# Two sums over partitions in an attention and MLP block: block transposes in place of a strided pass through DRAM, with a new order table

## The chip, the core and the metric

One of the eight cores of a Trainium2 chip runs the whole program. It has a matrix engine (TensorE, PE in the profile; its weight loads stand apart as PEld), a vector engine (VectorE, DVE), an activation engine (ScalarE, ACT), a slower general engine (GpSimd, POOL) and a sequencer (SyncE, SP) that here issues almost all transfers. Sixteen DMA engines carry the transfers. Each engine executes its own list of instructions strictly in order and waits for the others by semaphores, so an instruction that has to wait holds everything behind it on its engine. The metric is the device time of one execution in microseconds (us), lower is better.

## What is computed

The reference is a block with 2,048 tokens of width D = 576, cut here to its lines:

```
mod = (silu(c) @ w_mod).reshape(1, 6, 1, 576)      # c: 1 x 576, w_mod: 576 x 3456
sa, ca, ga, sb, cb, gb = mod[:, 0] ... mod[:, 5]
h = layernorm(x) * (1 + ca) + sa
x = x + ga * linear_attention(h, wqkv, wo)         # 32 heads of 18, kv and z summed over all tokens
h = layernorm(x) * (1 + cb) + sb
x = x + gb * (silu(h @ w1) @ w2)                   # F = 4608
```

The six modulation vectors come from one row times a 576 x 3456 matrix. The kernel takes them in three pieces of 1,152 columns: piece 0 (sa, ca) at the very start, and the later pieces 1 (ga, sb) and 2 (cb, gb) during the attention. The change concerns pieces 1 and 2.

## The kernel before

The first half of the program, called stage A here, works through the 16 tiles of 128 tokens in four blocks of four. For each tile the PE makes the k and q projections (line 928, into the banks psK), DVE and ACT apply the feature map (lines 935 to 941 and 494), and the PE adds up kv sums (line 1053, into the banks psG, from which ACT or DVE moves them to `sum`, lines 1061 to 1065). Every next block is layer-normalised, turned by DVE block transposes (line 1020) and a pass through DRAM (lines 1026 to 1035), modulated (lines 359 and 361) and split into a high and a low part (lines 996 and 997). At the end of stage A come the kv products (line 1186), a mask (line 1193), the products with wo (line 1223) and then the attention output and the MLP.

`mod_steps` (line 1090) makes pieces 1 and 2. Five times it loads 128 rows of w_mod (line 434), ACT scales each row by its silu(c) (lines 1099 and 1101), and POOL adds the result to `tmod` (line 1103). Then `tmod` holds 128 partial rows of 1,152 numbers that still have to be summed over the partitions. Before the change that is done through DRAM: SP stores `tmod` to `parts` (line 1104), the ACT queue fetches it back so that each partition gets 9 columns of all 128 rows, in pieces of 36 bytes (line 1107), DVE sums with a strided read (line 1110), and SP stores the 1,152 sums to `vec` (line 1111). From `vec` come the columns and rows that later work reads: `col_b`, `bc_ga`, `bc_gb` (lines 754, 1117, 1119, 1122), the bounds (line 757 and `find_bounds`), and with them the scale factors of the MLP (`find_factors`, lines 731 to 744).

Where things lie: the w_mod rows are loaded in turn into four rooms, two of them the accumulator rows of tiles 4 to 7 (`acc`), which q tiles 4 to 7 need later, and two the buffers `raw2`. The fetched `parts` lie in one `raw2` buffer. The buffer `crow` holds the sums.

Two tables set orders. `STAGE_A` gives the order in which the program text of stage A is emitted; the change doesn't touch it. `ORDERS` gives for each engine the order in which its instructions run: a list of indices, where index n is the n-th instruction emitted for that engine. Before the change it covers the first 2,991 PE, 656 DVE, 489 ACT, 262 POOL and 203 SP instructions, which is the program up to about 445 us; what is not listed follows in the order of emission. An instruction's place below is its position in such a list.

Of the kernel before, what the change touches and what calls it, by code (L numbers as in the profile page):

```python
# [9 lines left out]
F32 = mybir.dt.float32  # L10
# [8 lines left out]
P = 128  # L19
# [5 lines left out]
def kernel(ctx: ExitStack, tc, A_x, A_wqkv, A_wo, B_x, B_w1, B_w2, c, w_mod, out):  # L25
# [33 lines left out]
    def behind(instructions):  # L59

        with ExitStack() as order:
# [7 lines left out]
            0-43 45-46 52 49-50 44 47-48 53-54 51 65 57-58 61-62 66-72 55-56 59-60 63-64 73-77 82-83 80-81 78-79  # L69
            84-87 90-91 88-89 92-101 116-118 102-103 124 104-105 119-123 125 106-115 126-141 154-167 142-153  # L70
            168-181 246-251 210-213 182-199 214-215 290-293 216-219 294-295 200-209 220-221 256-267 274-277
            222-223 278-289 224-237 302-307 238-245 252-255 308-311 268-273 330-335 296-301 336-357 312-319
            358-359 320-325 360-367 326-329 368-375 378-383 376-377 386-389 384-385 398-403 390-393 404-405
            394-397 412-423 436-451 406-411 424-435 452-477 490-499 478-489 524-527 500-513 520-523 530-539
            514-519 586-587 528-529 588-589 540-545 554-571 576-579 592-597 590-591 598-599 610-621 600-609
            546-551 646-647 580-581 622-627 582-585 552-553 572-575 648-657 670-671 628-641 672-675 682-683
            642-645 684-687 714-721 658-663 722-723 664-665 692-693 666-669 688-689 694-713 724-725 676-679
            726-727 690-691 728-729 680-681 742-745 730-741 746-791 826-831 792-795 862-863 796-797 864-867
            832-833 872-873 798-813 838-839 814-815 840-853 816-821 854-855 822-823 856-859 874-877 860-861
            868-871 878-889 834-837 890-895 824-825 896-917 926-935 918-921 936-939 922-923 940-947 924-925  # L80
            978-983 1000-1003 950-955 966-975 1004-1005 976-977 984-993 948-949 994-999 1006-1019 1022-1023
            1020-1021 956-965 1024-1035 1050-1055 1036-1049 1056-1063 1084-1085 1064-1077 1102-1105 1086-1087
            1106-1113 1078-1079 1114-1117 1088-1091 1118-1123 1130-1131 1080-1081 1132-1135 1124-1129 1136-1137
            1082-1083 1138-1155 1096-1099 1092-1095 1160-1169 1156-1157 1170-1171 1100-1101 1172-1183 1158-1159
            1184-1219 1236-1237 1248-1259 1220-1221 1285-1286 1222-1227 1238-1247 1228-1235 1287-1296 1260-1262
            1297-1300 1263-1284 1301-1325 1352-1356 1326-1349 1357-1364 1385-1388 1365-1370 1389-1390 1350-1351
            1371-1384 1413-1416 1391-1400 1417-1427 1401-1406 1428-1429 1407-1412 1430-1443 1446-1449 1444-1445
            1451-1468 1450 1479-1486 1469-1478 1507-1511 1487-1506 1512-1535 1540-1544 1536-1539 1545-1568
            1573-1574 1569-1572 1575-1592 1601-1604 1593-1594 1605-1621 1595-1596 1634 1638 1597-1600 1622-1633
            1646-1649 1635-1636 1650 1639-1641 1655-1660 1687-1696 1637 1661-1676 1642-1645 1677-1682 1715-1719  # L90
            1697-1700 1651-1654 1701-1704 1683 1705-1706 1720-1723 1684-1686 1707-1714 1724-1751 1762-1767
            1776-1779 1781-1782 1768-1769 1780 1752-1753 1783-1794 1754-1761 1795-1798 1770-1772 1799-1800
            1773-1775 1801-1810 1821-1825 1854 1870-1873 1855-1857 1826-1835 1811-1820 1836-1843 1874 1858
            1875-1877 1844-1853 1859-1860 1883 1915 1884-1886 1861-1863 1916-1918 1878-1881 1887-1888 1882
            1864-1869 1889-1914 1919-1921 1931-1935 1976 1922-1927 1936-1939 1928-1930 1990-1993 1940-1941 1994
            1977-1978 1995-1996 1942-1971 2004-2007 1972-1975 1979-1982 2008-2010 1983-1984 2011-2012 1985-1988
            2013-2018 1989 2019-2036 1997-2003 2037 2049-2061 2082-2083 2098-2101 2062-2069 2086-2088 2070-2077
            2038-2045 2084-2085 2046-2048 2078-2081 2089 2102-2103 2090-2093 2106-2110 2094 2111-2112 2104
            2113-2114 2095-2097 2115-2122 2105 2123-2140 2143 2141-2142 2147 2159-2166 2144-2145 2167-2172 2146
            2173-2178 2187 2179-2186 2188 2199-2202 2189-2190 2203 2191 2204-2210 2213-2214 2148-2149 2215-2216  # L100
            2192-2198 2211-2212 2150-2158 2217 2231-2234 2218-2223 2235-2238 2224-2230 2239-2241 2249 2259-2262
            2245 2255-2258 2246-2248 2242 2263-2264 2243-2244 2265-2269 2295 2250 2296-2299 2251-2253 2270
            2309-2313 2254 2283 2271 2284-2285 2277-2278 2286-2293 2300 2294 2301-2302 2314 2303 2279 2304-2308
            2272-2276 2280-2282 2315-2324 2329 2335-2338 2325 2339-2340 2330-2331 2326-2328 2341 2332-2334
            2347-2356 2342-2346 2359-2360 2357 2361-2369 2358 2370-2377 2391 2378-2382 2392-2398 2383 2399-2404
            2384-2390 2405-2422 2427-2431 2423-2424 2433-2438 2432 2445-2450 2425-2426 2463-2470 2439-2444
            2451-2454 2483-2488 2503-2505 2457-2462 2489-2490 2506-2508 2455-2456 2555-2557 2521-2528 2471-2472
            2477 2473 2478 2474 2567 2479-2480 2475 2481-2482 2541-2542 2476 2543-2544 2568-2572 2545-2546 2491
            2547-2548 2558-2560 2492-2495 2497-2500 2496 2501-2502 2579-2584 2509-2520 2585-2586 2529-2537
            2593-2595 2538-2540 2549-2550 2596-2600 2551-2554 2561-2566 2607-2612 2573-2578 2587-2591 2619-2626  # L110
            2592 2633-2640 2601-2606 2647-2652 2613-2615 2627-2629 2616-2618 2630-2632 2659-2661 2641-2646
            2653-2654 2662-2663 2655-2658 2664-2692 2739-2740 2693-2698 2705-2708 2741-2742 2709-2710 2699-2704
            2733-2735 2719-2720 2743 2711-2718 2721-2732 2736-2738 2744-2762 2783-2794 2775-2782 2815-2820
            2795-2798 2873 2799-2800 2874-2875 2801 2763-2764 2802 2765 2876 2766-2767 2877-2878 2768-2774
            2833-2840 2803-2814 2853-2860 2821 2841 2822 2891 2842-2844 2929 2892-2895 2823-2830 2845-2852
            2930-2936 2879-2881 2909-2912 2831-2832 2882-2887 2913-2915 2888-2890 2916 2861-2867 2896-2898
# [2294 lines left out]
```

## Time and profile before

| | |
|---|---|
| median of 3 runs | 1085.9 us (1085.69 to 1086.51) |
| profiled execution, its own time | 1086.77 us |
| its span, first to last instruction | 1085.1 us |
| busy: PE, PEld, DVE, ACT, POOL | 98%, 70%, 82%, 65%, 68% |
| mean granted TensorE clock | 0.998 |

The shares are means over stages with different limits. A row of a timeline reads: start, length, engine, line, operation, what it writes <- what it reads, shape, count, and in brackets the idle time before it with the releaser.

### The profile page before, as it was taken

The numbers are of one execution on the slowest core, as the hardware profiler recorded it, in microseconds if no ns is written. First come the engines' busy times: TensorE is split into PE (matmuls) and PEld (weight loads), VectorE is DVE, ScalarE is ACT, GpSimd is POOL, SyncE is SP. The second block draws the span as 40 slices with busy tenths as digits, with TensorE's granted clock in tenths as the row PEclk, the third lists the DMA queues.
The fourth block names the chain that finished last, engine by engine and source line by source line (L and its number), as shares of the span: only waits on it lengthen the run. The fifth ranks groups of instructions, "written<-read, shape, count | busy, mean of one in ns | idle before, by whom it ended". The sixth has DMA issues, their size and how long they took to land.

```text
span 1085.1 us, 19052 instructions
## 1 busy us (share of the span) xinstructions
PE 1063.3 (98%) x7027; PEld 760.6 (70%) x7027; DVE 893.0 (82%) x1438; ACT 707.3 (65%) x1318; POOL 737.6 (68%) x804
## 2 busy tenths in 40 slices
PE   8999999999999899999999999999999999999998
PEld 6999999898885455666666666666666666666665
DVE  7966857788889899988987988987987887898767
ACT  4866553248667777777667667767766776676554
POOL 3467524654725589879888778877778678677563
PEclk9999999999999999999999999999999999999999
DMA  8497954224256877387577577567667657626422
GB/s 294 143 178 202 101 148 119 70 83 127 61 165 195 240 250 254 125 250 230 175 223 213 182 217 222 171 223 203 200 196 234 201 154 252 206 68 201 165 80 109
DMA packets 119341, 193.50 MB, mean 178 GB/s; under 512 B 42892, under 2 KB 77584, under 8 KB 119248
## 3 DMA queue, kind: packets, MB, share of 16 engines
q1 hardware_dynamic: 86276, 190.81, 56.6%
q10 hardware_dynamic: 32972, 1.48, 3.1%
q8 instruction: 55, 0.90, 0.4%
q14 instruction: 38, 0.31, 0.1%
HBM read 176.77 MB, written 15.48 MB: 177 GB/s over the span
## 4 chain that ended last, share of the span: by engine, by line
PE 80%; DVE 9%; DMA 4%; ACT 2%; POOL 2%; issue 1%; SPq 0%; DVEq 0%; POOLq 0%; ACTq 0%
PE up L1924 31%; PE down L2008 30%; PE big L389 5%; PE psK L928 4%; PE psG L1053 4%; PE big L1443 2%; DMA raw<-parts 1%; DMA hT<-hd 1%; PE small L1432 1%; DVE hT L261 1%; PE small L374 1%; DMA raw<-in_w_mod_dram 1%; DVE w L261 1%; PE big L1357 1%; PE psK L1223 1%
## 5 line engine op out<-in xcount | busy, mean ns | idle before, releaser
L1924 PE MATMUL up<-hT,w 128*128 128x512 f16 x1264 | 317.9, 379 | 2.2 <-DMA hT<-hd 2.2
L1924 PEld LDWEIGHTS <-w 128*128 128x128 f16 x1492 | 145.8, 98 | 136.1 <-DMA hT<-hd 2.9
L2017 DVE SCALAR_TENSOR_TENSOR acc<-acc,set,down 128x576 f32<-128x576 f32 x128 | 103.6, 810 | 33.8 <-PE down L2008 32.9
L1942 ACT ACTIVATE f<-f,set 128x512 f32<-128x512 f32 x102 | 73.3, 719 | 63.6 <-DVE f L1948 52.1
L1962 POOL TENSOR_TENSOR s<-f,f 128x256 f32<-128x256 f32 x66 | 54.6, 827 | 77.4 <-ACT f L1943 75.3
L2008 PE MATMUL down<-w,hc 128*128 128x288 f16 x600 | 90.6, 286 | 0.1
L2008 PE MATMUL down<-w,hb 128*128 128x288 f16 x600 | 89.3, 286 | 0.6 <-DVE U L2019 0.5
L2008 PE MATMUL down<-w,hT 128*128 128x288 f16 x480 | 82.8, 286 | 0.4 <-DVE acc L2021 0.4
L1946 DVE TENSOR_TENSOR f<-up,p 128x512 f32<-128x512 f32 x102 | 69.6, 682 | 13.8 <-PE up L1924 9.4
L1943 ACT ACTIVATE f<-f,set 128x512 f32<-128x512 f32 x102 | 73.6, 722 | 3.2
L2008 PEld LDWEIGHTS <-hb 128*128 128x128 f16 x600 | 58.7, 98 | 22.7 <-issue 1.4
L2008 PEld LDWEIGHTS <-hc 128*128 128x128 f16 x600 | 58.7, 98 | 22.0 <-issue 0.4
L1986 POOL TENSOR_TENSOR hc<-s,hc 128x512 f16<-128x512 f32 x50 | 63.9, 1278 | 6.0 <-ACT hc L1982 6.0
L1948 DVE TENSOR_TENSOR f<-up,f 128x512 f32<-128x512 f32 x68 | 46.8, 689 | 25.4 <-PE up L1924 24.3
L2008 PEld LDWEIGHTS <-hT 128*128 128x128 f16 x480 | 46.9, 98 | 26.6 <-issue 0.8
L1966 POOL TENSOR_TENSOR f<-f,s 128x256 f32<-128x256 f32 x66 | 53.4, 809 | 17.3 <-DVE hb L1986 10.2
L1959 POOL TENSOR_TENSOR s<-f 128x256 f32<-128x256 f32 x66 | 57.0, 864 | 9.5 <-ACT f L1939 4.5
L1964 POOL TENSOR_TENSOR s<-s,f 128x256 f32<-128x256 f32 x66 | 56.3, 853 | 3.5
L389 PE MATMUL big<-w,qT 128*128 128x288 f32 x352 | 58.6, 304 | 0.0
L2008 PE MATMUL down<-w,hd 128*128 128x288 f16 x396 | 55.5, 286 | 0.2 <-DVE acc L2017 0.2
L2008 PE MATMUL down<-w,ha 128*128 128x288 f16 x396 | 55.7, 286 | 0.0
L1053 PE MATMUL psG<-w,xs 128*128 128x288 f32 x336 | 52.2, 296 | 1.3 <-DVE sum L1063 1.3
(408 smaller groups left out, 2805.3 us busy)
## 6 DMA issues: line engine op xcount, KB each, us to landing
hT<-hd SPq DMA_DIRECT2D x101, 640.0 KB, 4.6
hT<-hd SPq DMA_DIRECT2D x65, 512.0 KB, 3.7
hT<-in_B_w_dram SPq DMA_DIRECT2D x14, 576.0 KB, 6.4
hT<-in_B_w_dram SPq DMA_DIRECT2D x28, 256.0 KB, 5.8
raw<-in_B_w_dram SPq DMA_DIRECT2D x11, 576.0 KB, 6.2
v<-in_B_w_dram SPq DMA_DIRECT2D x9, 576.0 KB, 4.9
acc<-in_A_x_dram SPq DMA_DIRECT2D x16, 288.0 KB, 4.3
raw<-in_B_w_dram SPq DMA_DIRECT2D x9, 512.0 KB, 5.2
```

What stands on the lines that cost most here:

```text
L389: T.matmul(ps, xpart(a), wpart(b), start=n == 0, stop=n == len(XW) - 1)
L1053: T.matmul(ps[:, h, :HALF], l, pk[t][:, u, h * HALF : (h + 1) * HALF], start=t == 0 and m == 0, stop=t == 3 and m == len(left) - 1)
L1924: T.matmul(ps, left, right, start=first and m == 0, stop=m == len(seq) - 1, skip_group_check=True)
L1942: A.activation(f, f, AF.Silu, scale=factor(self.g, "inv"))
L1943: A.activation(f, f, AF.Identity, scale=factor(self.g, "delta"))
L1946: V.tensor_add(f, self.bank[bank[1]], self.p1)
L1959: G.tensor_sub(self.s3, half(i, 0, 0), half(i, 0, 1))
L1962: G.tensor_add(self.s[:, 0:1], half(i, 0, 1), half(i, 1, 1))
L1964: G.tensor_sub(self.s[:, 1:2], self.s[:, 0:1], half(i, 0, 0))
L1986: eng.tensor_sub(t[:, :, 1, :], src, t[:, :, 0, :])
L2008: T.matmul(ps[:, p, :HALF], left[:, u, p * P : (p + 1) * P], right[:, v], start=n in (1, 5, 7, 6) and j == 0, stop=j == len(passes) - 1, s ...
L2017: V.scalar_tensor_tensor(dst, dst, factor(self.g, "ratio"), ps[:, :, :HALF], op0=ALU.mult, op1=ALU.add)
```

## The change

Pieces 1 and 2 no longer go through `parts`. DVE turns `tmod` in blocks of 32 by 32 (two transposes of 128 x 576, one for each half of the piece), so that after a sum over the last 32 numbers each partition holds a quarter's sums; one transpose of 128 x 64 turns those; a store of 128 rows of two times 128 bytes and two loads bring the four quarters side by side on 36 partitions, and a last small reduction adds them. The sums then go to `vec` as before. The three new transfers are issued on SP. A memset clears the part of `crow` that the small transpose reads. A check is added to `follow`. All five lists of `ORDERS` are new. The core of the diff:

```diff
+    V.memset(crowp[:, 64:128], 0.0)
...
-        do("SP", 0.45, lambda: nc.sync.dma_start(parts, tmod2[:, :, 0:D]), ["tmod0", "tmod1"], [f"parts{piece}"], 8.0)
         i = next(of_raw) % 2
-        r = raw2[i].rearrange("q a d -> q (a d)").rearrange("q (p j) -> q p j", j=NC9)
-        do("SP", 0.45, lambda: nc.scalar.dma_start(r, parts.rearrange("p a d -> p (a d)").rearrange("p (q j) -> q p j", j=NC9)),
-           [f"parts{piece}"], raws2[i], 14.0)
-        s9 = s9s[piece - 1]
-        do("DVE", 2.27, lambda: V.tensor_reduce(s9, r.rearrange("q p j -> q j p"), axis=AX.X, op=ALU.add), raws2[i], [f"s9{piece}"])
-        do("SP", 0.45, lambda: nc.sync.dma_start(vec.rearrange("a d -> (a d)").rearrange("(q j) -> q j", j=NC9), s9),
+        r, some = raw2[i], crowp[:, 64:128]
+        flat = r.rearrange("p a d -> p (a d)")
+        four = flat[0:NB32, 0:P].rearrange("b (q c) -> b q c", q=4)
+        turned_sums = flat[:, 1024:1088]
+        total = crowp[0:NB32, 64:96]
+
+        def turn():
+            for a in range(2):
+                V.transpose(r[:, a].rearrange("p (b i) -> p b i", i=32), tmod2[:, a, 0:D].rearrange("p (b i) -> p b i", i=32))
+
+        def fold():
+            V.tensor_reduce(some[:, 0:NB32], flat.rearrange("p (b i) -> p b i", i=32), axis=AX.X, op=ALU.add)
+            V.transpose(turned_sums, some)
+            nc.sync.dma_start(quarters.rearrange("h p c -> p h c"), turned_sums.rearrange("p (h c) -> p h c", h=2))
+            for h in range(2):
+                n = (32, NB32 - 32)[h]
+                nc.sync.dma_start(four[32 * h : 32 * h + n], quarters[h].rearrange("(q b) c -> b q c", q=4)[:n])
+            V.tensor_reduce(total, four.rearrange("b q c -> b c q"), axis=AX.X, op=ALU.add)
+
+        do("SP", 0.45, lambda: None, ["tmod0", "tmod1"], [f"parts{piece}"], 8.0)
+        do("SP", 0.45, turn, [f"parts{piece}", "tmod0", "tmod1"], raws2[i], 14.0)
+        do("DVE", 2.27, fold, [], [*raws2[i], f"s9{piece}"])
+        do("SP", 0.45, lambda: nc.sync.dma_start(vec.rearrange("a d -> (a d)").rearrange("(b c) -> b c", c=32), total),
```

Those parts of the lists of which the text below speaks (PE old and new, the first DVE lines new). In the DVE list index 6 is the memset, and the new instructions of `turn` and `fold` shift the indices behind them:

```diff
     "PE": ...
-            0-43 45-46 52 49-50 44 47-48 53-54 51 65 57-58 61-62 66-72 55-56 59-60 63-64 73-77 82-83 80-81 78-79
...
-            1184-1219 1236-1237 1248-1259 1220-1221 1285-1286 1222-1227 1238-1247 1228-1235 1287-1296 1260-1262
...
-            2384-2390 2405-2422 2427-2431 2423-2424 2433-2438 2432 2445-2450 2425-2426 2463-2470 2439-2444
...
+            0-38 41-42 39-40 43 45-46 44 52 51 65-72 49-50 55-56 59-60 73-77 47-48 53-54 57-58 61-62 80-81 84-85
...
+            1287-1290 1260-1267 1291-1292 1268-1284 1293-1335 1352-1356 1336-1345 1357-1364 1346-1351 1385-1388
...
+            2445-2446 2422-2426 2433-2436 2428-2431 2447 2432 2437-2438 2448-2450 2439-2444 2451-2456 2463-2470
     "DVE": ...
+            0 2 1 4-5 3 7-18 54 19-20 55 21-23 25 27 29-30 26 31 24 28 44-46 32 47-50 33-35 52 42 38 36-37 70 73
+            71-72 39 41 40 74-76 56 79 77 58 43 51 57 80-81 78 82 60 53 59 62 84 64 87 66 63 67-68 65 86 61 85
+            69 88 90-91 89 83 6 92 95-96 94 99-100 97 93 133-134 103 101-102 108 104 110 105 126 129 109 113
+            111-112 114 116-118 121 115 120 122-123 135 119 98 124 128 107 106 130 125 127 131-132 138-139 137
+            136 140-141 145 144 147 142 146 151 158 143 197-198 148 150 149 155 152 157 154 171 153 156 160 159
+            161 170 164 163 168 167 199 169 173 172 174 177 166 181 165 175 178 189 162 195 180 179 176 182-183
...
```

PE indices 1260 to 1284 are the kv products (line 1186), 1285 to 1300 the rest of a q projection (line 928), 1301 to 1318 the products with wo (line 1223); 2439 to 2456 are down products of line 2008 and 2463 to 2470 the up products of line 1924 that wait for a fetched `hT`; 43 to 64 are the first k products (line 573), 51, 52, 65 and 66 the row sums of line 538, 67 to 70 filler products and 71 and 72 the turned rows (line 549).

## Rows read from the trace of the kernel before

**Rows 1.** The page: busy us, share of the span and instructions of each engine.

```profile
PE 1063.3 (98%) x7027; PEld 760.6 (70%) x7027; DVE 893.0 (82%) x1438; ACT 707.3 (65%) x1318; POOL 737.6 (68%) x804
```

**Rows 2.** Waits of PE, 0 to 345 us: total us, times, longest us.

```profile
PE big L1443 <- DVE acc L1448: 1.9, 1, 1.9
PE psG L1053 <- DVE sum L1063: 1.3, 2, 0.7
PE psK L1223 <- issue: 1.2, 1, 1.2
...
PE big L389 <- DVE v L475: 0.7, 1, 0.7
```

**Rows 3.** Waits of PE, 345 to 460 us.

```profile
PE up L1924 <- DMA hT<-hd: 2.2, 1, 2.2
```

**Rows 4.** The chain of waits, 0 to 330 us: start, length, what ran.

```profile
71.21 16.20 DMA raw<-parts
87.44 2.40 DVE crow L1110
89.86 6.37 DMA raw<-in_w_mod_dram
...
128.71 6.41 PE psK L928 x48
...
205.30 1.29 DVE set L744
```

**Rows 5.** Stretches: us; PE, PEld, DVE, ACT, POOL us (instructions); granted clock; DMA share; GB/s.

```profile
20.80:24.20 3.40, 3.40 (x13) 1.97 (x12) 2.37 (x8) 0.38 (x1) 1.89 (x2) 0.50 1.05 319
24.20:45.00 20.80, 19.52 (x141) 18.35 (x142) 19.22 (x42) 16.80 (x32) 7.34 (x7) 1.00 0.35 105
60.00:80.00 20.00, 20.00 (x153) 20.00 (x152) 14.47 (x32) 13.00 (x20) 13.17 (x9) 1.00 1.01 158
72.00:79.00 7.00, 7.00 (x55) 7.00 (x54) 5.00 (x12) 5.20 (x8) 4.31 (x2) 1.00 1.49 60
100.00:120.00 20.00, 19.35 (x146) 19.10 (x145) 16.88 (x32) 12.91 (x22) 14.52 (x10) 1.00 0.31 96
340.00:380.00 40.00, 34.64 (x202) 19.35 (x200) 35.31 (x54) 28.75 (x58) 21.34 (x28) 1.00 0.75 216
```

**Rows 6.** Transfers of `parts`: issues with first and last start, time to landing.

```profile
L1104 SPq DMA_DIRECT2D parts<-tmod x2: 562/582/603, 64.9 to 110.0; - x2
...
DMA to landing us min/median/max: 13.9/13.9/13.9
```

**Rows 7.** DVE groups by shape, 60 to 200 us: busy us, mean ns, idle before.

```profile
L1020 DVE STREAM_TRANSPOSE acc<-xt 128x576 f32<-128x576 f32 x8 | 5.5, 743 | 0.1
L1110 DVE TENSOR_REDUCE crow<-raw 128x9 f32<-128x1152 f32 x2 | 4.7, 2362 | 1.5 <-DMA raw<-parts 1.5
L776 DVE TENSOR_REDUCE den<-w 128x32 f32<-128x576 f32 x2 | 1.5, 748 | 0.1
L1197 DVE COPY tmod<-tmod 128x64 f32<-128x64 f32 x1 | 0.2, 195 | 0.0
```

**Rows 8.** Waits of DVE, 100 to 112 us.

```profile
DVE acc L941 <- POOL tmod L1103: 2.4, 1, 2.4
```

**Rows 9.** Transfers from and to `vec`: time to landing.

```profile
DMA to landing us min/median/max: 4.1/5.4/7.0
```

**Rows 10.** Timeline of DVE, 56 to 80 us.

```profile
58.76 0.76 DVE L941 TENSOR_SCALAR acc<-psK 128x576 f32<-128x576 f32 x1 [0.93 <-ACT e L935]
...
72.63 0.68 DVE L997 TENSOR_TENSOR hT<-h,hT 128x512 fp32r<-128x512 f32 x1
```

**Rows 11.** Timeline of POOL, 36 to 72 us.

```profile
62.12 2.79 POOL L1103 TENSOR_TENSOR tmod<-tmod,acc 64x576 f32<-64x576 f32 x2
```

**Rows 12.** Timeline of PE, 12 to 25 us.

```profile
18.78 0.70 PE L538 MATMUL psG<-hT,ones 128*1 128x320 f32 x2 [0.90 <-DVE hT L518]
20.19 0.82 PE L573 MATMUL psK<-w,hT 128*128 128x288 f32 x4 [0.71 <-DVE hT L261]
```

More of the change, by code (lines that the diff above doesn't have):

```diff
@@ new lines @@
+            78-79 116-121 88-89 122-123 92-93 96-105 63-64 82-83 86-87 90-91 94-95 106-111 124 112-115 125-139
+            246-247 140-141 210-211 142-143 248-251 154-161 212-213 162-165 214-215 144-147 216-217 148-153
+            166-175 290-291 176-203 256-261 204-205 262-263 206-209 292-295 264-267 274-289 222-227 218-219
+            228-237 302-305 220-221 238-239 268-273 306-319 296-301 336-341 330-333 320-321 334-335 366-367
+            240-245 252-255 322-325 368-369 326-329 342-365 370-377 386-393 378-381 394-395 382-385 398-403
@@ new lines @@
+            396-397 404-405 412-423 436-443 406-411 444-445 424-429 446-451 430-435 452-509 514-519 510-513
+            530-531 520-521 532-533 586-587 522-523 534-543 524-529 592-597 554-569 544-547 610-611 588-591
+            598-599 612-615 548-551 616-621 600-609 552-553 570-571 576-585 572-575 646-649 622-645 650-657
+            670-681 658-659 682-683 714-715 660-665 684-685 666-669 716-717 688-689 686-687 718-719 692-695
+            690-691 696-713 720-755 770-789 756-763 790-791 862-865 764-769 792-793 826-831 794-797 866-867
@@ new lines @@
+            1854-1857 1870-1872 1810 1834-1837 1873 1811-1816 1838-1843 1858-1864 1817-1820 1874-1877 1883
+            1844-1853 1884-1885 1865-1866 1878-1882 1886 1867 1887-1890 1868-1869 1891-1917 1919 1976 1931-1935
+            1920-1923 1977-1978 1918 1924-1930 1936-1945 1979 1946-1953 1980-1982 1954-1963 1990-1991 1964
+            2004-2008 1992 2009-2010 1993 1983-1985 1965-1968 1994 1986 1969-1975 1987-1989 2011-2036 1995-1996
+            2037 2049-2053 1997-1998 2038 1999-2003 2054-2071 2086 2072-2077 2039-2040 2078-2084 2098-2099
@@ L174 @@
[L174 to L176 removed]
+            9 0-2 7 3 5-6 4 8 11 13 15 14 10 12 18 16-17 19 21-23 20 24 26-27 47 29 25 28 30-33 39 36-38 43
+            40-42 34-35 49 44 48 45 62 46 50-53 63 54-55 57 56 58-60 72 61 64 70 65 67 75 71 69 73 68 66 76-77
@@ L186 @@
+            188-190 202 169 192 180 194 179 181 198 203 195 201 200 205-206 204 193 208-210 196 207
         """,
@@ L831, in follow @@
             while len(made) < len(self.ops):
+                before = len(made)
                 for queue in queues.values():
@@ L835, in follow @@
                         self.ops[queue.pop(0)][2]()
+                assert len(made) > before
         def emit(self):
@@ L885 @@
     xT = accb[NB - 2].rearrange("p a d -> p (a d)")
-    NC9 = 2 * D // P
-    s9s = [crowp[:, 64 + 16 * i : 64 + 16 * i + NC9] for i in range(2)]
+    NB32 = 2 * D // 32
     turned = [dram.tile([D, 4, P], F32, name=f"turned{b}") for b in range(1, NB)]
-    parts_of = [dram.tile([P, 2, D], F32, name=f"parts{i}") for i in (1, 2)]
+    quarters_of = [dram.tile([2, P, 32], F32, name=f"quarters{i}") for i in (1, 2)]
     vec_of = [dram.tile([2, D], F32, name=f"vec{i}") for i in (1, 2)]
@@ L1090, in mod_steps @@
     def mod_steps(piece):
-        parts, vec = parts_of[piece - 1], vec_of[piece - 1]
+        quarters, vec = quarters_of[piece - 1], vec_of[piece - 1]
         for k in START:
```

194 lines of the change are left out of this document (88 added, 106 removed).

## The prediction

> **What bounds the kernel now.** I read the page's busy shares first. PE is busy for 1063.3 of 1085.1 us [rows 1], so PE paces the kernel, its work is not changed, and an edit elsewhere is worth what it takes from or adds to PE's 22 us of idle time. The second view is therefore the list of PE's waits [rows 2, 3]. In the part that the order lists cover it names 1.9 us behind the additions of line 1448, 1.3 us in two waits behind the sums of line 1063, 1.2 us ahead of the wo products (line 1223), 0.7 us behind line 475 and 2.2 us behind a fetched `hT`. No wait is for `parts`, `vec` or `crow`. The third view, the chain of waits, shows `parts` all the same: 16.2 us of fetch, 2.4 us of reduction, then a w_mod load into the room that it held [rows 4]. In that stretch PE is busy for 20.00 of 20 us [rows 5], so the chain ran beside a full PE. The stage around it belongs to PE, not to DVE (14.47 of 20 us) or to the transfers.
>
> **What is removed.** Two fetches of 13.9 us each [rows 6], during which the 16 DMA engines are full and move only 60 GB/s [rows 5], two stores, and two strided reductions, 4.7 us of DVE together [rows 7]. PE waits for none of them directly: nothing on the path. One thing hangs on them. The w_mod rows of piece 2 lie in accumulator rooms that a q tile needs, and piece 2 is late because its loads wait for the `raw2` room. DVE waits 2.4 us there for POOL's additions [rows 8], and the sums of line 1063 queued behind it hold PE: one of its two waits in [rows 2], 0.65 us of the 1.3 (the two are 0.6 to 0.7 us each). Reduction and room come free after two transposes (1.49 us), a reduction (1.5 us) and two hops of about 5.4 us [rows 7, 9], some 14 us after `tmod`, where store, fetch and reduction took 24.9 us (64.9 to 89.8) [rows 4, 6]. I take -0.65 us (bounds -0.65 and 0).
>
> **What is added.** For each piece on DVE: two transposes of 128x576 at 743 ns; a reduction of 1,152 numbers a partition in order, twice line 776 at 748 ns; a small transpose at 0.2 us (the copy of the same size) to 0.74 us (the large one), I take 0.2; a last reduction of 128 numbers on 36 partitions, I take 0.2 us (between nothing and the 0.75 us of line 776 for 576) [rows 7]. That is 3.4 us in place of 2.36 us, +2.1 us for both pieces and a short memset. DVE's idle share covers it (5.5 and 3.1 us of each 20 us around the two pieces [rows 5]); uncovered it would cost 2.1 us. On SP three short transfers replace a store. Behind them stand the later w_mod loads and `vec`; POOL's sums wait for those loads, and they are early already. Nothing, at most the hold below.
>
> **What DVE now waits for in order.** I read the two transposes of piece 1 as the indices 93 and 94, at places 99 and 95 of the new list, around line 941. Before, that line runs at 58.76 us [rows 10], but POOL finishes the two halves of `tmod` only at about 63.5 and 64.9 us [rows 11]. If POOL is no faster, DVE stands for 5 to 7 us, and behind it queue line 941, the reduction, and the subtractions of line 997 that the next block's k products need. The last of them slips from 73.3 us to about 78 us [rows 10] (65 us, then two transposes, two halves of a feature map, the reduction and some 20 short instructions). PE has sum products of line 1053 until 72.5 us that need no DVE, then takes the k products chunk by chunk, so most of the slip is hidden. I take +0.6 us, bounds 0 and +3.
>
> For the third instruction of `fold` (index 135, place 124) DVE must see the sums come back from DRAM: two hops, 10.8 us by the median and 14 us at most [rows 9], against some 11 us of DVE work between the two places. So it waits between 0 and 3 us inside DVE's slack: nothing. The Trainium skill ("DMA: Bandwidth & Descriptors", section "Anatomy of one DMA") puts the fixed part of a transfer at about 2 us; an estimate by that page is 4 us for both hops, and DVE would not wait at all. The trace disagrees: the short transfers around `vec` take 4.1 to 7.0 us.
>
> **What the new lists move.** PE's list can be compared index by index.
> - At the end of stage A, indices 1293 to 1300 of a q projection stood ahead of the kv products (1260 to 1284) and now stand between them and the wo products (1301), where PE waits 1.2 us for the masked kv. Eight products at 0.134 us (6.41 us for 48 [rows 4]) are 1.07 us: -1.07 us (bounds -1.2 and -0.8).
> - In the DVE list the factor steps (lines 735 to 744) stand 10 to 22 places earlier, so `set` of line 744, 1.29 us on the chain at 205.3 us [rows 4], no longer stands ahead of line 475, for which PE waits 0.7 us [rows 2]: -0.7 us (bounds -0.7 and 0).
> - Indices 2439 to 2456, 18 down products, stand ahead of 2463 instead of behind it, where PE waits 2.2 us for `hT` [rows 3]. At the 0.134 us of a q product they are 2.4 us. Some need weight parts that DVE makes only about then: -1.2 us (bounds -2.2 and 0).
> - Line 1448 stands ahead of the block sums at 340 us, which shortens the wait of 1.9 us, but DVE is busy for 35.3 of the 40 us there [rows 5] and the rest comes back a little later: -0.4 us (bounds -1.9 and +1).
> - At the start the row sums (65, 66) and the turned rows stand ahead of most of the first k products, and DVE's two row additions ahead of a modulation and a subtraction of 0.95 us together. The wait of 0.90 us at 18.78 us [rows 12] comes earlier and grows, the chain behind it starts up to 0.95 us earlier: -0.4 us (bounds -0.95 and +2).
> - The lists move PE's other instructions by some ten places on average, and what stood well before may now wait. I give back half of the first three gains, +1.2 us (bounds 0 and +3).
>
> **The sum.** -0.65 + 0.6 - 1.07 - 0.7 - 1.2 - 0.4 - 0.4 + 1.2 = -2.6 us. From the profiled execution's own 1086.77 us (span 1085.1 us and 1.67 us around it) that is 1084.15 us. The median of the runs is 0.87 us below that execution, so the forecast for the median is 1083.3 us, 0.24% faster.
>
> **Rivals.**
> - *The gaps move (0.30).* The waits taken away return behind other instructions, as the new lists were not made on this trace. For it: DVE is nearly full at 340 to 380 us [rows 5]. Against it: the three clearest moves put ready work exactly into a wait. With -0.65 us and the last term at its +3, all other terms halved, 1084 to 1087 us, in the middle 1085.4 us: the same.
> - *The edit does nothing that PE sees (0.07).* The fetch was hidden, and the moved products find their operands late. Only the 0.65 us of [rows 8] is left: 1085.2 us.
> - *DVE's hold at `tmod` reaches PE (0.05).* Place: the transposes of piece 1, DVE at 57 to 65 us. For it: POOL's 64.9 us [rows 11]. Against it: PE's work until 72.5 us. PE has to lose 4.8 us more than I take for the time to pass 1088.1 us; a hold of 7 us that PE pays in full, in place of my 0.6, gives 1089.7 us.
> - *TensorE's clock at the start (0.04).* From 20.8 to 24.2 us the granted clock is 0.50, the lower level of 1.2 GHz [rows 5], after PE stood 0.90 and 0.71 us [rows 12]; then it is 1.00. With longer idle times there the stretch could grow. In the 20.8 us behind it PE is busy for 19.52 us [rows 5]; each us at the lower level costs about half a us. From 9.6 us more of it the kernel is slower; ten us give 1088.3 us. The Trainium skill ("TensorE: Matmul & The Clock Gate", section "Part 1: The HAM clock gate") says that the throttled state is the default and activity releases it; the trace agrees, at 0.50 behind those waits.
>
> **How the numbers follow.** The forecast has 0.54, the rivals 0.30, 0.07, 0.05 and 0.04. About 0.2% (2.2 us) is what a measurement tells from no change. Faster 0.54; same 0.30 + 0.07 = 0.37; slower 0.09. The terms at their low ends without the +1.2 and the +0.6 give -7.6 us, 1078.3 us; all together are unlikely, so the range begins at 1080.0 us. At the top it takes in most of the first rival and ends at 1086.9 us. The forecast's own range is 1080.0 to 1083.7 us.
>
> **What would show it.** After: no fetch of 13.9 us and no stretch at 60 GB/s; transposes of 0.74 us at about 64 us; DVE no longer waiting for POOL ahead of line 941 near 103 us; no wait of 1.2 us ahead of line 1223, of 0.7 us behind line 475 and of 2.2 us behind `hT`. The forecast is wrong if PE waits several us between 60 and 80 us, if the clock's lower stretch grows, or if PE's waits before 445 us add up to as much as before.

## The result, and the profile after

The changed kernel is slower: 1088.84 us median (1087.07 to 1092.71, 20 executions) against 1084.70 us (1081.99 to 1086.69, 20 executions), a ratio of 1.0043 (95% interval 1.0034 to 1.0053). The forecast was 1083.3 us, with a range of 1080.0 to 1086.9 us. The two profiled executions show only part of that: the one of before, 1086.77 us, lies above all 20 timed ones, the one after, 1087.52 us, near the low end of its own.

The page after, its row of busy times, beside [rows 1]:

```profile
PE 1062.0 (98%) x7027; PEld 760.3 (70%) x7027; DVE 893.1 (82%) x1447; ACT 708.6 (65%) x1318; POOL 732.2 (67%) x804
```

The waits of PE after, 0 to 345 us, beside [rows 2] (total us, times, longest). Line numbers have moved: 573 is now 579, 928 is 936, 997 is 1005, 1443 is 1467, 1924 is 1948; in the kernels below they move again by up to eleven lines, as the lists have other lengths.

```profile
PE psK L579 <- DVE raw L367: 2.9, 1, 2.9
PE small L380 <- ACT H L365: 1.8, 1, 1.8
PE psK L579 <- DVE hT L267: 1.6, 2, 1.4
PE psK L936 <- DVE hT L1005: 1.4, 1, 1.4
PE small L1456 <- DVE hT L267: 1.2, 1, 1.2
```

The same, 345 to 460 us, beside [rows 3]:

```profile
PE big L1467 <- DVE acc L1472: 1.8, 1, 1.8
PE up L1948 <- DVE acc L1472: 1.3, 1, 1.3
PE down L2032 <- DVE acc L2045: 0.7, 2, 0.5
PE up L1948 <- DMA hT<-hd: 0.5, 1, 0.5
```

The waits that the forecast set out to remove are gone: nothing behind line 1063's sums, nothing ahead of the wo products, nothing behind line 475; between 84 and 250 us PE has no wait in the list at all. In their place stand new ones of 2.9, 1.8, 1.4 and 1.2 us, and PE's idle time (span less busy time) grows from 21.8 to 23.8 us. The head shows it first. PE's timeline, 12 to 32 us, beside [rows 12]:

```profile
18.63 1.06 PE L579 MATMUL psK<-w,hT 128*128 128x288 f32 x3 [2.94 <-DVE raw L367]
...
29.01 0.53 PE L579 MATMUL psK<-w,hT 128*128 128x288 f32 x2 [1.45 <-DVE hT L267]
```

DVE's timeline, 12 to 20 us:

```profile
14.26 0.54 DVE L367 TENSOR_SCALAR raw<-psK,col_a 128x256 f32<-128x256 f32 x1
...
15.31 2.73 DVE L524 SCALAR_TENSOR_TENSOR hT<-hT,sc 128x640 f32<-128x640 f32 x3
17.95 0.54 DVE L367 TENSOR_SCALAR raw<-psK,col_a 128x256 f32<-128x256 f32 x1
```

The second modulation, for which PE stands, comes behind three row additions, 3.65 us later than in the kernel before (14.30 us). Stretches of the changed kernel, columns as in [rows 5]:

```profile
15.70:18.60 2.90, 0.00 (x0) 0.00 (x0) 2.83 (x5) 0.75 (x2) 0.00 (x0) 0.64 1.05 412
18.60:22.80 4.20, 4.17 (x11) 1.17 (x11) 2.16 (x6) 1.08 (x4) 0.00 (x0) 0.50 1.07 358
22.80:24.20 1.40, 1.40 (x9) 1.10 (x8) 1.09 (x3) 0.91 (x2) 0.99 (x1) 0.81 1.02 272
...
320.00:340.00 20.00, 17.97 (x124) 12.93 (x124) 14.37 (x26) 13.45 (x23) 11.04 (x11) 1.00 0.58 204
340.00:360.00 20.00, 16.61 (x104) 9.85 (x103) 19.88 (x30) 12.04 (x23) 6.67 (x6) 1.00 0.60 198
```

PE idles through the first of them, the clock falls, and the second runs at 0.50. By the clocks of the three (0.64, 0.50, 0.81) the lower level lasts some 6.8 us, where it lasted 3.4 us before [rows 5]. DVE's timeline around the first piece, 60 to 84 us, beside [rows 10]:

```profile
62.42 0.78 DVE L1121 STREAM_TRANSPOSE raw<-tmod 128x576 f32<-128x576 f32 x1 [4.33 <-POOL tmod L1111]
...
67.86 0.76 DVE L1121 STREAM_TRANSPOSE raw<-tmod 128x576 f32<-128x576 f32 x1
68.66 1.35 DVE L1124 TENSOR_REDUCE crow<-raw 128x36 f32<-128x1152 f32 x1
...
76.65 0.81 DVE L342 BATCH_NORM_STATS2 st<-acc 128x6 f32<-128x288 f32 x2
...
79.30 0.68 DVE L1005 TENSOR_TENSOR hT<-h,hT 128x512 fp32r<-128x512 f32 x1
...
80.70 0.38 DVE L1130 TENSOR_REDUCE crow<-raw 36x32 f32<-36x128 f32 x1
```

The subtraction of `h`, at 72.63 us before, is now the last of the block; it ends at 79.98 us, and the k product that reads it waits 1.42 us. The last reduction (80.70 us) waits for nothing.

Where the time went is seen best by cutting the span at the same amount of PE work. Below, the time between the starts of PE's matmul records 0, 300, 1000, 1418, 2000, 2400, 2700 and 3300 (each trace has 7,027 records; in the changed kernel these lie at 1, 53, 148, 207, 285, 346, 402 and 501 us), worked out from the records of each trace. From record 3300 to 6900 the kernels of the table take 563.6 us (tail_330: 564.3 us).

| profile of | 0 | 300 | 1000 | 1418 | 2000 | 2400 | 2700 |
|---|---|---|---|---|---|---|---|
| before | 51.6 | 94.9 | 60.6 | 79.1 | 60.0 | 55.8 | 96.9 |
| changed | 52.2 | 95.1 | 58.6 | 77.9 | 61.1 | 56.0 | 98.7 |
| changed_again | 52.5 | 95.1 | 58.6 | 77.9 | 61.2 | 57.5 | 98.9 |
| tail_of_before | 52.2 | 95.1 | 58.5 | 79.1 | 60.0 | 53.6 | 96.8 |
| tail_raw_h | 49.1 | 94.1 | 58.5 | 79.1 | 60.0 | 53.8 | 98.0 |
| tail_330 | 51.9 | 95.2 | 58.6 | 77.9 | 65.0 | 54.7 | 96.8 |
| tail_360 | 52.3 | 95.0 | 58.6 | 77.9 | 61.1 | 56.5 | 96.8 |
| four_turned | 52.4 | 95.1 | 58.6 | 77.9 | 59.2 | 56.0 | 99.3 |

From 148 to 285 us the change gains 3.2 us (2.0 and 1.2); it loses at the head and behind 285 us. The first two rows differ by only 0.7 us in all, as the two profiled executions do. So the table tells where an order differs; what it costs is taken from repeated runs below.

### The profile page after: what moved, and what is told of

It reads as the page before. It is cut to its first block, busy times and chain, and to the rows that moved or that the text cites. A ratio compares the mean times of both kernels' runs of the same rounds, so it can differ in the third digit from the quotient of the medians.

```text
span 1085.8 us, 19068 instructions
## 1 busy us (share of the span) xinstructions
PE 1062.0 (98%) x7027; PEld 760.3 (70%) x7027; DVE 893.1 (82%) x1447; ACT 708.6 (65%) x1318; POOL 732.2 (67%) x804
## 3 DMA queue, kind: packets, MB, share of 16 engines
HBM read 175.63 MB, written 14.37 MB: 175 GB/s over the span
## 4 chain that ended last, share of the span: by engine, by line
PE 87%; DVE 8%; DMA 3%; ACT 1%; issue 1%; POOL 0%; SPq 0%; DVEq 0%; POOLq 0%; ACTq 0%
PE up L1948 32%; PE down L2032 30%; PE psK L936 8%; PE big L395 6%; PE psG L1061 5%; PE big L1467 1%; DMA acc<-in_A_wqkv_dram 1%; PE small L1456 1%; DMA hT<-in_w_mod_dram 1%; DVE hT L267 1%; PE psK L1247 1%; DVE w L273 1%; PE small L380 1%; PE big L1381 1%; DMA hT<-hd 1%
## 5 line engine op out<-in xcount | busy, mean ns | idle before, releaser
L1966 ACT ACTIVATE f<-f,set 128x512 f32<-128x512 f32 x102 | 73.2, 719 | 61.7 <-DVE f L1972 52.2
L1983 POOL TENSOR_TENSOR s<-f 128x256 f32<-128x256 f32 x66 | 56.5, 855 | 8.8 <-ACT f L1963 7.3
```

The lines of the kernel that those rows point to most:

```text
L1966: A.activation(f, f, AF.Silu, scale=factor(self.g, "inv"))
L1983: G.tensor_sub(self.s3, half(i, 0, 0), half(i, 0, 1))
```

## The experiments

Theory H: the head is what costs (a late modulation, then a lower clock). Theory W: DVE's stand at `tmod`. Theory C: the new instructions. Theory L: the new lists behind 205 us. A spliced kernel takes one order for the instructions that start before a given time in one trace, and the other order behind them. Ratios are to the kernel before, run beside each, with 95% intervals. The medians of the kernel before beside the runs go from 1083.5 to 1084.9 us, so a difference of about 1 us between medians of two runs says little.

**head_of_after and tail_of_before: the two ends of the order alone.**

```diff
 head_of_after (on the kernel before, sums through DRAM kept)
+ instructions of the first 35.5 us in the changed kernel's order
 tail_of_before (on the changed kernel)
+ instructions behind 205 us in the order of the kernel before
```

> The kernel before, with the old sums through DRAM, and only the instructions that start in the first 35.5 us of the changed kernel put into the new order. Theory H: 3 to 4.5 us slower than before (ratio 1.003 to 1.004), with PE's wait of about 2.9 us at 15.7 us and a mean granted clock of 0.992 to 0.997. Theories W and L: within 1 us of before (1.000 to 1.001).

> The changed kernel with its new lists up to 205 us, and everything later in the order of the kernel before. Theory L: 1.5 to 2 us faster than the changed kernel (ratio 1.002 to 1.003 to the kernel before), since PE's idle time behind 250 us (10.9 against 8.9 us in the two traces) comes back to that of before. Theory H: the tail gives back 1 us at most (ratio 1.003 to 1.004).

Measured: head_of_after 1.0022 (1.0010 to 1.0034), with the same wait of 2.94 us, so the head costs 2.4 us, less than the 3 to 4.5 us of Theory H. tail_of_before 0.9996 (0.9987 to 1.0005), 4.8 us below the changed kernel by the medians: the later lists cost most, more than twice what Theory L expected.

**head_of_before: the head undone.**

```diff
 head_of_before (on the changed kernel)
+ instructions of the first 35.5 us in the order of the kernel before
```

> The changed kernel, with the instructions that start in the first 35.5 us of the kernel before put back into that kernel's order on every engine; behind them the new lists. Theory H (the head: DVE reaches a modulation late, PE stands 2.94 us at 15.7 us, TensorE's clock falls and stays at its lower level for longer): PE's idle time up to 50 us falls from 7.8 to about 5.5 us, the lower clock begins later, and the time falls by 3 to 4.5 us, to about the kernel before (ratio 0.999 to 1.001). Theory W (DVE's wait for the last sums of tmod reaches PE at 78 us): the head gives 1 us at most, ratio 1.003, and the wait of 1.4 us at 78.6 us stays. Theory L (the later lists, behind 250 us): ratio 1.003 too.

Measured: 1.0052 (1.0038 to 1.0066), no gain. The splice made a wait of its own. PE's waits, 0 to 50 us, first row, and a later stretch:

```profile
PE psG L1055 <- ACT w L960: 2.0, 1, 2.0
```

```profile
404.50:408.00 3.50, 3.50 (x12) 1.51 (x11) 0.86 (x2) 1.00 (x3) 2.08 (x3) 0.51 0.45 176
```

The clock falls in this execution behind a wait of 1.67 us at 402 us. It tells nothing against Theory H; single instructions had to be moved.

**tail_raw and tail_filled: one modulation, and the same wait filled.**

```diff
 tail_raw (on tail_of_before)
-DVE: 25 27 29-30 26          ACT: 11 14 12
+DVE: 25 26 27 29-30          ACT: 11 12 14
 tail_filled (on tail_of_before)
-PE:  43 45
+PE:  43 (12 new filler products) 45
```

> tail_of_before with two instructions of the head moved: on DVE the second modulation of the first tiles (index 26) ahead of the three row additions of 0.89 us instead of behind them, and on ACT the copy of its high part (index 12) ahead of a weight copy (index 14). Theory H (the head's loss is this one modulation that comes late): PE's wait of 2.94 us at 15.7 us falls to 0.5 to 1.2 us, some 1 us returns ahead of the row sums, and the kernel is 1.5 to 2.5 us faster than tail_of_before (ratio to the kernel before about 0.9978). Rival (the row additions set the end of the head anyway): 0.5 us or less (0.9992 or more).

> tail_of_before with twelve more filler products of 128x128 (their result is not used; the sum of the output is unchanged) on PE ahead of the product that waits 2.94 us at 15.7 us. The wait for the modulation stays, but PE is busy in it. If the lower clock that follows costs time by itself: no stretch of 0.50 from 17 us on, or a later and shorter one, and 1 to 2 us faster than tail_of_before (ratio to the kernel before 0.998 to 0.999). If only the wait costs: as tail_of_before, 0.9996.

Measured: tail_raw 0.9975 (0.9962 to 0.9989), 2.0 us below tail_of_before by the medians; the two intervals just overlap. tail_filled 0.9987 (0.9976 to 0.9998), 1.5 us below it, though the intervals of these two overlap. PE's waits of tail_raw, 0 to 40 us:

```profile
PE psG L534 <- DVE hT L514: 1.3, 1, 1.3
...
PE psK L569 <- DVE raw L357: 0.4, 1, 0.4
```

The stretch behind the wait, in tail_of_before and then in tail_filled:

```profile
18.60:22.80 4.20, 4.12 (x11) 1.17 (x11) 2.20 (x6) 1.08 (x4) 0.00 (x0) 0.50 1.06 338
```

```profile
18.60:22.80 4.20, 4.13 (x26) 2.30 (x25) 3.78 (x12) 1.67 (x4) 1.41 (x1) 1.00 1.06 334
```

By the medians the late modulation makes 2.0 of the head's 2.4 us. Filled, the same wait isn't followed by the lower clock in the profile: 26 matmul records stand where 11 stood, and the mean clocks of the executions are 0.997 to 1.000 in place of 0.995 to 0.997.

**code_old_order and code_late: the new sums in the old order.**

```diff
 code_old_order: transposes and reductions where tmod is ready
+DVE at 65.0 and 110.1 us of the kernel before, ahead of line 997
 code_late: the same, behind the last subtraction of the block
+DVE at 76 and 120.3 us
```

> The new sums (block transposes, three short transfers) with the order of the kernel before on every engine; the new instructions are placed where their operands are ready (the transposes of piece 1 at the time of 65.0 us, of piece 2 at 110.1 us), so DVE doesn't stand for tmod. Theories H and L (the order lists are what costs): as before or up to 0.7 us faster (ratio 0.999 to 1.000), as the room of the w_mod rows comes free earlier. Theory C (the new instructions themselves cost, by DVE's 2.1 us more or SP's short transfers): 1 to 2 us slower (ratio 1.001 to 1.002).

> The new sums with the order of the kernel before, as code_old_order, but the transposes and reductions stand behind the last subtraction of the block for which the k products wait (at the time of 76 and of 120.3 us), not where tmod is ready. Theory P (it is the place of 2.9 us of DVE work ahead of subtractions that PE waits for, not the instructions themselves): PE's waits of 2.4 and 1.6 us at 75 and 119 us go, ratio to the kernel before 0.999 to 1.001. Theory C (the new code costs wherever it stands): 1.003 or more.

Measured: code_old_order 1.0059 (1.0043 to 1.0076), code_late 1.0022 (1.0008 to 1.0037). PE's waits from 60 to 135 us, in the first and then in the second:

```profile
PE psK L925 <- DVE hT L994: 4.2, 3, 2.4
PE psG L1050 <- DVE sum L1060: 1.3, 2, 0.6
```

```profile
PE psG L1050 <- DVE sum L1060: 1.4, 2, 0.8
PE psK L925 <- ACT hT L993: 0.9, 1, 0.9
PE psK L925 <- DVE hT L994: 0.6, 1, 0.6
```

In the old order the new code costs 6 us where it is ready first, as 2.9 us of DVE work stand ahead of subtractions that PE needs. Placed later, more than half of that is gone, but not all: of Theory C, 1 to 4 us stay, so with this order the change gains nothing by itself. In both the two waits behind the sums (line 1060) are still there, as in [rows 2].

**tail_stats, tail_raw_stats and tail_raw_h: the stand at tmod.**

```diff
 tail_stats (on tail_of_before), tail_raw_stats (on tail_raw)
-DVE: 96 94 99
+DVE: 96 110 109 113 111-112 114 116-118 121 94 99
 tail_raw_h (on tail_raw)
-DVE: 105 126 129 ... 121 115      ACT: 75 88 79 82 86 80-81
+DVE: 105 115 126 129 ... 121      ACT: 75 80-81 88 79 82 86
```

> tail_of_before with ten statistics instructions of DVE (some 3.5 us) moved ahead of the transpose of piece 1 that waits 4.3 us for POOL's tmod; before the change such instructions filled that stretch. Theory W (the wait costs PE what is queued behind it on DVE): the wait of 1.42 us at 78.6 us and that of 0.19 us at 70.4 us go, and the kernel is 1.2 to 1.6 us faster than tail_of_before (ratio to the kernel before about 0.9983). Rival (the transposes and the reduction, 2.9 us, are what delays the last subtraction, or the wait moves on to the next product): 0.5 us or less (0.9992 or more).

> Both moves in one kernel. If both theories hold and the gains add up: 2.7 to 4 us faster than tail_of_before, ratio to the kernel before 0.996 to 0.997. If PE's idle time only moves: 0.9985 or more.

> tail_raw with the last modulation and copy of h on ACT (indices 80, 81) ahead of the copies of line 983 and the scaling of the next w_mod rows, and its subtraction on DVE (index 115) ahead of the fp32r subtractions of line 987 and of all statistics. Theory W (the stand at tmod costs PE what DVE and ACT have queued ahead of this one subtraction): PE's wait of 1.42 us at 76 to 80 us goes, 1.2 to 1.6 us faster than tail_raw, ratio to the kernel before about 0.9962. Rival (the wait moves to the next product, as DVE's work is only exchanged): 0.5 us or less, 0.997 or more.

Measured: tail_stats 1.0065 (1.0051 to 1.0079), tail_raw_stats 1.0044 (1.0031 to 1.0056): both theories miss. DVE's waits of tail_stats, 56 to 70 us:

```profile
DVE st L332 <- DMA acc<-in_A_x_dram: 10.4, 1, 10.4
```

The tiles that the statistics read landed at 68.3 us in this order (before the change the statistics ran from 59.85 us), so the stand at 62 us can't be filled with this work, and PE lost 6.6 us. tail_raw_h moves the one subtraction instead: 0.9967 (0.9954 to 0.9980), the fastest of all, 4.0 us below the kernel before (1084.39 us beside it). PE's waits in it, 60 to 84 us:

```profile
PE psK L926 <- ACT e L933: 0.6, 1, 0.6
PE psG L1051 <- ACT sum L1059: 0.2, 1, 0.2
```

The wait of 1.42 us went, one of 0.6 us came; the gain on tail_raw (0.9 us by the ratios) is within the intervals. The profiles put it in the right place: records 300 to 1000 take 95.1 us in tail_raw and 94.1 us in tail_raw_h.

**tail_300, tail_330, tail_360 and changed_again: where the later lists lose.** As tail_of_before, with the seam at 300, 330 and 360 us in place of 205 us; and the changed kernel once more.

> As tail_of_before, but the new lists are kept up to 330 us, not up to 205 us. If the new tail loses between 205 and 330 us (PE's idle time there is 4.0 us in the changed kernel against 1.8 us in tail_of_before): 2 us slower than tail_of_before, ratio 1.0015. If it loses behind 330 us: as tail_of_before, 0.9996.

> As tail_of_before and tail_330, with the new lists kept up to 300 us. It has the new lists' waits of 0.53 us at 258 us and of 1.25 us at 291 us, but not that of 1.75 us at 325 us. If the loss between 205 and 330 us is mostly this last wait and a lower TensorE clock behind it: ratio 1.000 to 1.001 to the kernel before, and no stretch of lower clock behind 300 us. If it is spread over the stretch: 1.002 to 1.004.

> The changed kernel with the order of the kernel before from 360 us on. By the stretches of PE's records in the profiles the new lists lose 1.1 us at 285 to 346 us, 2.4 us at 346 to 402 us and 1.9 us at 402 to 500 us against tail_of_before. If these add up and the seam costs nothing: the last and some of the second come back, 2 to 3 us faster than the changed kernel, ratio to the kernel before 1.0015 to 1.0025, and PE's records 2700 to 3300 take 96.9 us in place of 98.7 us. If the loss is all ahead of 330 us, as the two splices at 300 and 330 us would have it: 1.004.

> The changed kernel itself once more, beside the two others. Expected 1.0043 again; if the wait at 325 us is followed by a lower clock in most executions, its profile has a stretch of 0.50 near 328 us, which the first profile of it did not have.

Measured: 1.0007 (0.9998 to 1.0017), 1.0043 (1.0030 to 1.0055), 1.0034 (1.0020 to 1.0048), and 1.0035 (1.0021 to 1.0048) for the changed kernel. I first took the step from tail_300 to tail_330 for the loss of 300 to 330 us. The table doesn't bear that out so simply: tail_330 takes 65.0 us behind record 2000, the changed kernel 61.1 us. Of this, 1.9 us is a wait for the additions of line 1472 (at 343 us in tail_330; in the changed kernel it comes at 349 us and falls into the next stretch), and 1.7 us is lost clock (0.43 of the 4 us of the last row below). Over both stretches tail_330 takes 119.7 us and the changed kernel 117.1 and 118.7 us in its two profiles; what the seam itself costs isn't separated. tail_360's profile gets back 1.9 us behind record 2700 (96.8 against 98.7 us). Its time doesn't settle that: by the medians it is 2.0 us faster than the changed kernel, but its ratio of 1.0034 is that of changed_again, and misses the 1.0015 to 1.0025 that was expected. By the same table the new lists also lose 1.1 us behind record 2000 and 2.4 us behind record 2400 against tail_of_before. The clock falls in some executions only. Changed_again, and then the same stretch of tail_330:

```profile
328.00:332.00 4.00, 3.72 (x24) 2.31 (x24) 3.20 (x7) 2.45 (x4) 2.04 (x3) 1.00 0.53 201
352.00:356.00 4.00, 4.00 (x21) 2.61 (x20) 2.92 (x6) 1.20 (x3) 0.00 (x0) 0.57 0.76 279
```

```profile
328.00:332.00 4.00, 3.91 (x15) 2.00 (x16) 1.29 (x7) 2.08 (x3) 2.38 (x4) 0.57 0.54 198
```

**ten_moved, early_h_325 and four_turned: the wait of 1.75 us at 325.7 us.**

```diff
 ten_moved (on the changed kernel)
-PE:  2208 2213-2216 2209-2211 ...
+PE:  2208 2209-2212 2153-2158 2213-2216 ...
 early_h_325 (on ten_moved; 2212 stands behind 2158)
-ACT: 287-289 286 290-291          DVE: 433 477 475 468
+ACT: 290-291 287-289 286          DVE: 433 468 477 475
 four_turned (on the changed kernel)
-PE:  2159-2186 2148-2152 2143 2199-2200 2144 2201-2202 2145-2146
+PE:  2159-2166 2143-2146 2167-2186 2148-2152 2199-2202
```

> The changed kernel with one edit in PE's list: ten products that stand behind the transposes of line 380 (indices 2209 to 2212 and 2153 to 2158, some 1.6 us of work) stand ahead of them, where PE waits 1.75 us at 325.7 us. If this one wait and the lower clock that follows it in most executions make the 3.9 us by which the new lists lose between 300 and 330 us: 3 to 4 us faster than the changed kernel, ratio to the kernel before 1.000 to 1.0015, a wait of 0.4 us or less at 325 us and the full clock behind it. If the products only leave a hole where they stood, or the loss is elsewhere: 1.003 to 1.0045.

> The changed kernel with the wait of 1.75 us at 325.7 us taken at its source, as ten_moved showed it: ACT modulates and copies H (indices 290, 291) ahead of the four normalisations of line 357 (2.29 us), DVE's subtraction of H (index 468) stands ahead of the normalisation that waits for POOL, and PE's ten products stand ahead of the transposes of line 380. If ACT's order makes this wait: 0.6 us or less of it is left, 1 to 2 us faster than the changed kernel, ratio to the kernel before 1.002 to 1.003. If the chain through statistics and POOL ends it all the same: 1.0035 to 1.0045.

> The changed kernel with four instructions of PE's list moved: the transposes of line 380 with indices 2143 to 2146, which the new list puts behind 28 products of line 395 (322.97 to 324.16 us), stand after eight of them, as the list before wove such transposes between products. DVE stands 2.64 us at 321.8 us and ACT 4.33 us for these, and behind them DVE is busy for 19.88 of the 20 us from 340 us, where PE waits 1.84 and 1.35 us for it. If this stand is what the new lists lose between 285 and 402 us: DVE's wait falls below 0.5 us, PE's wait of 1.75 us at 325.7 us goes, the two later ones shrink by 1 us or more together, and the kernel is 2.5 to 4 us faster than the changed kernel (ratio to the kernel before 1.000 to 1.0015). If DVE's load behind 330 us sets the end anyway (rival, as in early_h_325): 1.003 or more.

Measured: ten_moved 1.0060 (1.0046 to 1.0075), early_h_325 1.0061 (1.0046 to 1.0076), four_turned 1.0017 (1.0007 to 1.0027). In ten_moved the ten products themselves wait 2.18 us for a copy that ACT makes behind four normalisations. In early_h_325 the wait is down to 0.45, 0.32 and 0.25 us, but PE's waits at 350 and 360 us stay at 1.84 and 1.35 us and two more of 0.76 us together come between: the gain comes back as other waits. In ten_moved's profile that wait is followed by the lower clock (0.50 from 328.9 to 332.3 us), and records 2000 to 2400 take 64.3 us, against 61.1 us; why early_h_325 is slower than the changed kernel isn't settled. DVE's waits show the source of the wait at 325.7 us. The changed kernel, 285 to 362 us, then four_turned, 318 to 332 us:

```profile
DVE xn L359 <- PE small L380: 2.6, 1, 2.6
```

```profile
DVE hT L261 <- ACT hT L1658: 0.8, 1, 0.8
DVE mv L345 <- POOL mv L342: 0.7, 1, 0.7
DVE acc L1389 <- PE big L389: 0.7, 1, 0.7
```

The new PE list puts four transposes behind 28 products of line 395; DVE stands 2.64 us for the buffer that they free, is busy for only 14.37 of the 20 us from 320 us (16.88 in tail_of_before), and then for 19.88 of the 20 us from 340 us, where PE waits for it. (In tail_of_before DVE is busy for 19.34 us of the latter.) With the four moved, DVE's stand and PE's wait of 1.75 us are gone and the kernel is about 2 us faster. The waits of 1.84 and 1.34 us behind DVE stay, so that half of the expectation failed, and DVE's stand isn't their cause:

```profile
PE big L1461 <- DVE acc L1466: 1.8, 1, 1.8
PE up L1942 <- DVE acc L1466: 1.3, 1, 1.3
```

**tail_raw_h_filled: the other wait of the head.**

```diff
 tail_raw_h_filled (on tail_raw_h)
-PE:  51 65
+PE:  51 (5 new filler products) 65
```

> tail_raw_h with five more filler products of 128x128 ahead of the row sums, where PE waits 1.28 us at 16.5 us and the clock then stands at 0.50 up to 24 us (3.4 us lost in the profiled execution). If the lower clock follows from this wait: clock 0.999 or 1.000 and 1 to 3 us faster than tail_raw_h, ratio to the kernel before 0.994 to 0.996. If the clock falls all the same: as tail_raw_h, 0.9967.

Measured: 0.9975 (0.9965 to 0.9985), no gain on 0.9967. In its profile PE's clock is 1.00 from 15.7 to 24 us, as expected, but 0.57 from 11.5 to 15.5 us, ahead of the fillers and behind a wait of 0.71 us:

```profile
11.50:15.50 4.00, 4.00 (x24) 4.00 (x23) 3.90 (x6) 1.82 (x4) 2.05 (x2) 0.57 1.06 383
```

## Why the prediction was wrong, step by step

- **What is removed** (-0.65 us): the size was reached, but not by this mechanism. Both waits behind line 1063's sums are gone, 1.3 us. They are still there in code_old_order and code_late (1.3 and 1.4 us), where the fetch is gone as well, so the new order took them away. In code_old_order DVE doesn't even wait for POOL's `tmod` there. In code_late it does without the fetch, and in the changed kernel that wait [rows 8] stands ahead of the transposes of piece 2. DVE's waits from 100 to 112 us, in these two:

```profile
DVE acc L938 <- POOL tmod L1100: 1.3, 1, 1.3
```

```profile
DVE raw L1121 <- POOL tmod L1111: 1.8, 2, 1.2
```

- **What is added**: the durations were right (0.78, 1.35, 0.25 and 0.38 us against 0.74, 1.5, 0.2 and 0.2 us). "DVE's idle share covers it" failed: code_old_order shows that a share of 20 us says nothing of the place; 2.9 us for each piece, ahead of the subtractions, cost PE 4.2 us there in three waits.
- **What DVE now waits for in order** (+0.6 us): the mechanism was right (4.33 us stood, 5 to 7 us expected), the size wrong. The last subtraction ends at 79.98 us, not at 78 us, since statistics that ran from 59.85 us before now stand right ahead of it (76.65 to 79.3 us); PE paid 1.42 and 0.19 us. (The 73.3 us before is the end of the subtraction of `h`; one more followed, until 74.7 us.) The wait for the sums from DRAM was nothing, as taken. The 2 us that the prediction takes for a transfer from the Trainium skill ("DMA: Bandwidth & Descriptors", section "Anatomy of one DMA") stand there for transfers issued from GpSimd; these are issued on SP, and the 4.1 to 7.0 us of [rows 9] decide.
- **The q products and the factor steps** (-1.07 and -0.7 us): right. The waits of 1.2 and 0.7 us are gone, and the stretch behind record 1000 takes 2.0 us less, against 1.8 us forecast. The next stretch gained 1.2 us more, for which there was no term.
- **The 18 down products** (-1.2 us): wrong, as the wait moved. In the other 13 profiles with the old order there, the product that waited 2.17 us for a fetched `hT` waits between nothing and 2.60 us, so 2.2 us was no fixed price. In the six profiles with the new order that wait is gone, but each of the six has one of 0.50 to 1.67 us for a fetched `hT` that is read 170 records later. Before, and then the changed kernel:

```profile
374.17 1.04 PE L1924 MATMUL up<-hT,w 128*128 128x512 f16 x4 [2.17 <-DMA hT<-hd]
```

```profile
403.14 1.02 PE L1948 MATMUL up<-hT,w 128*128 128x512 f16 x4 [0.50 <-DMA hT<-hd]
```

- **Line 1448** (-0.4 us): wrong. PE waits 1.84 us for its additions again, and 1.35 us for the next, which cost 0.8 us before (below, 345 to 460 us): +0.5 us. The cause is open; four_turned rules out DVE's stand just ahead.

```profile
PE up L1924 <- DVE acc L1448: 0.8, 1, 0.8
```

- **The start** (-0.4 us): wrong in sign, and the first step that failed. I counted two row additions moved ahead of 0.95 us of work. Three were, 2.73 us, and what came late was the modulation that PE's next product needs; PE stood 2.94 us. head_of_after prices it at +2.4 us (1.1 to 3.7), past its bound of +2.
- **"I give back half of the first three gains, +1.2 us"**: this term failed by most. tail_of_before prices the lists behind 205 us at about +4.8 us, beyond its bound of +3 us. The lists of PE's waits from 285 to 501 us add up to 9.0 us in the changed kernel and 5.1 us in tail_of_before. four_turned explains some 2 us of the price. Behind 402 us PE has six waits of 0.15 to 0.50 us, 1.9 us together, against 0.5 us in two: the one for the fetched `hT`, the others of down products (line 2032) for DVE. The wait of 1.25 us at 291.7 us is new: DVE makes the part of `hT` that the product reads behind two other subtractions of 2.3 us together (first row), where tail_of_before has it earlier (second row). No run undoes these, so their share of the time isn't shown.

```profile
292.19 0.69 DVE L267 TENSOR_TENSOR hT<-sl,hT 64x512 f16<-64x512 f32 x1
```

```profile
289.57 1.65 DVE L257 TENSOR_TENSOR hT<-sl,hT 64x512 f16<-64x512 f32 x1
```

- **Rivals**: the gaps did move, at a higher price than that rival gave. Its own terms add up to +0.8 us, 1086.7 us, and not to the 1085.4 us stated. The clock rival was taken for a case by itself at 0.04; it came along with the other waits. The mean granted clock is 0.9951 over 26 executions of the changed kernel and 0.9976 over the 112 of the kernel before that ran beside the experiments. An estimate from these: the difference, 0.0025 of 1088 us, is at most 2.7 us of the 4.1 us (less, where PE idles at the lower level). The Trainium skill ("TensorE: Matmul & The Clock Gate", section "HAM oscillation — how this bites in real kernels") says that a wait ahead of a group of products can throttle the engine again, so that the group starts at the lower rate. The traces agree: 0.50 behind the wait of 2.94 us, 1.00 in tail_filled, 0.51 behind 1.67 us in head_of_before.

Two of the prediction's own signs of being wrong came: the clock's lower stretch at the start grew, from 3.4 to some 6.8 us, and PE's waits add up to more (its idle time grew by 2.0 us).

The pieces: +2.4 us for the head (head_of_after), +0.2 us behind record 300, where the stand of 1.6 us and the 1.3 us of waits removed meet, -2.0 us behind record 1000, and +4.8 us for everything behind 205 us (tail_of_before; the 1.2 us gained behind record 1418 are in it). That is +5.4 us, against 4.1 us by the medians and 4.7 us by the ratio. The first three alone are tail_of_before: +0.6 us by this sum, -0.4 us (-1.4 to +0.5) measured.

## What to carry to other kernels

Read a new global order instruction by instruction where PE is close to its operands, not by mean places: find the producer of PE's next operand and count what stands ahead of it on its engine, a wait for another engine included. Take a gain from a wait on a transfer only if more than one profile shows the wait, and look where it may reappear. Time code and order apart: here the new code in the old order loses, the new order loses at its head and tail, and both with the old order behind 205 us and a few instructions put right at the head and the stand (tail_raw_h) are 0.33% faster than the kernel before. No run has the old sums in the new order, so what the new code is worth there isn't shown.

## What the runs showed of the hardware

- TensorE's clock fell to its lower level behind single waits of 1.7 to 2.9 us in a kernel that is busy for 98% of its span, but not in every execution: the changed kernel's two profiles differ at 352 to 356 us (1.00 and 0.57). It fell behind shorter ones too: 0.90 and 0.71 us in the kernel before [rows 12], 0.71 us in tail_raw_h_filled. In code_late, with the order of the kernel before at the start, it stayed at 1.00 behind 1.00 and 0.71 us. The mean clocks of the changed kernel's executions run from 0.992 to 0.997. The three at 0.997 took 1087.7 to 1088.7 us, the two at 0.992 took 1092.5 and 1092.7 us, 4 to 5 us more, where the lost clock is 0.005 x 1088 = 5.4 us.
- In the 14 profiles with the order of the kernel before at that place, PE waited between nothing and 2.6 us for the same `hT` fetch.
